# A decode step on one core: wider PV matmuls, the first FFN weight as the moving operand, the second as rows only

## The chip, the core and the metric

The kernel runs on one core of one Trainium2 chip. The time is that of the device, in microseconds (us). TensorE is called PE (its weight loads PEld), VectorE DVE, ScalarE ACT, GpSimd POOL, and SyncE, which issues the transfers, SP (its queue SPq).

## The reference

Eight batch rows of one token (D = 448) pass through attention, a SiLU block, the same attention and the same SiLU block again, with residuals and LayerNorm without weights. Attention has 16 query heads on 8 key-value heads (head width 256) over the last 1024 of 4096 cached positions; the FFN width is 1792. All inputs are bf16.

```python
def _A_ref(x, k_cache, v_cache, wq, wo):
    ...
    W = min(4096, max(256, Sk // 4))
    rep = Hq // Hkv
    q = (lambda x, *d: x.transpose(*d))((x @ wq).reshape(B, Sq, Hq, Dh), 0, 2, 1, 3)
    k = jnp.repeat(k_cache[:, :, Sk - W:, :], rep, axis=1)
    v = jnp.repeat(v_cache[:, :, Sk - W:, :], rep, axis=1)
    scores = jnp.einsum("bhqd,bhkd->bhqk", q, k) * (Dh ** -0.5)
    p = _softmax(scores, axis=-1)
    o = jnp.einsum("bhqk,bhkd->bhqd", p, v)
    return (lambda x, *d: x.transpose(*d))(o, 0, 2, 1, 3).reshape(B, Sq, Hq * Dh) @ wo
...
x = A_x
x = x + _A_ref(_layernorm(x, axis=-1), A_k_cache, A_v_cache, A_wq, A_wo)
x = x + _B_ref(_layernorm(x, axis=-1), B_w1, B_w2)
x = x + _A_ref(_layernorm(x, axis=-1), A_k_cache, A_v_cache, A_wq, A_wo)
x = x + _B_ref(_layernorm(x, axis=-1), B_w1, B_w2)
```

`_B_ref` is `silu(x @ w1) @ w2`.

## The kernel before

Both attention calls read the same keys and values, so each batch row's cache (8 key and 8 value blocks of 512 KB) is brought in once and used twice. SP loads the blocks as 256 transfers of 256 KB, in the order keys, values, batch by batch, into 29 slots of SBUF. A transfer waits for the landing of the one seven before it (`AHEAD = 7`) and for its slot to be free. Key slots of a batch become free after its second layer's scores, value slots after its second layer's PV. The weights follow the first batch's values.

The outer loop runs over the eight batches; for each, `layer1(b)` and `layer2(b)` declare tasks, and a planner (`Plan.schedule`) orders all tasks of each engine by a list schedule with assumed durations. The order is then fixed: each engine runs its list in order and waits by semaphores. Where PE would be idle, the planner puts `fill` matmuls (L1045) that change nothing. So the second half of one batch runs among the first half of the next.

The steps of a batch, with the names that the profile and the change use:

- **KT** (L998, DVE): turns the key blocks 32 x 32 in place, 16 pieces of 512 words per batch.
- **scores** (L672, PE), the max over positions and its spread (L678 to L691, DVE), **exp** (L695, ACT), **pT** (L701, PE) and its copy (L709, ACT), the sums **l** over positions by eight matmuls with a matrix of ones (L712, PE), their reciprocal **rl** (L717, DVE).
- **PV** (`pv_rows`, L731): p as stationary operand (two columns), a value block of 256 columns as moving operand, four heads side by side in the four 32-column tiles of the array, added up over the eight blocks of positions. Then the eviction **oev** (L736, ACT), the turn into columns **oT** (L738, PE) and the division (L742, DVE).
- **wo** (`rows_part`, L774, and `cols_part`, L780): output product as rows in four tiles, the rest as columns; **fold** (L790 ACT, L791 PE) adds the four row tiles to the columns in bank YB.
- **up** (`up`, from L830): `xb_evac` (L801, L802), the statistic **s12** (`stat`, L808 to L813: four matmuls for the sum, four for the squares, one for epsilon), then DVE's reciprocal root (`rsqrt`), and **w1** (L833): 14 blocks of 128 x 128 of the weight as stationary operand, x as moving operand of 32 equal columns, for four parts of D. `vt`, `tanh`, `zh`, `hT` give silu.
- **chain** (`chain`, from L847): **w2** 8 parts as rows and 6 as columns, fold, the normalized row `xn`, the second statistic (its root on POOL), **wq** (L877) in four tiles, its turn **qT** (L882, DVE), `qsel` (L888, PE), `qbd` (L892, DVE); then the second layer's scores.

PSUM is used by whole banks: a task that writes a bank waits for all readers of that bank. `rowb`, the row that `fold` reads, is the first half of the buffer `qT`; the second layer's `e_sb` is its second half. The second layer's last FFN is done for seven batches at once in `final_rows` and for the last batch in `final_last`.

Of the kernel before, what the change touches and what calls it, by code (L numbers as in the profile page):

```python
# [280 lines left out]
def bass_interleave_layers__sliding_block_cached__dense_activation_silu__decode_kernel(  # L281
# [15 lines left out]
    F0 = 1024  # L297
# [33 lines left out]
    pT_sb = [sb(f"pT_sb{i}", [P, 2, 4, 16], BF16) for i in range(2)]  # L331
# [5 lines left out]
    o_sb = [sb(f"o_sb{i}", [P, DH], BF16) for i in range(2)]  # L337
# [9 lines left out]
    rowb = qT[:, 0:256].bitcast(BF16)  # L347
    ROWK = [("qT", 0)]
# [4 lines left out]
    xbt = sb("xbt", [P, KC + 1], BF16)  # L353
# [36 lines left out]
    C_L, C_O, C_Q, C_ST = 256, 320, 352, 480  # L390
    C_CV = 256
    C_XF = 256
    C_W1 = 64
# [3 lines left out]
    def bk(i):  # L397
        return [("bank", i)]
# [53 lines left out]
    pool(lambda e: e.memset(xbt[:], 0.0), [], [("xbt", i) for i in range(3)], 0.1)  # L452
# [14 lines left out]
    pool(lambda e: e.memset(w1_sb[64:128, 3 * F + F - F0:], 0.0), [], ["w1_pad"], 0.2)  # L467
# [25 lines left out]
    def load_w1():  # L493
        for c in range(3):
            dma(lambda e, c=c: e.dma_start(w1_sb[:, c * F:(c + 1) * F], B_w1[c * P:(c + 1) * P, :]),
                [("w1", c)], P * F * 2, "w1%d" % c)
        for h in range(2):
            n = (F0, F - F0)[h]
            dma(lambda e, h=h, n=n: e.dma_start(w1_sb[64 * h:64 * h + 64, 3 * F:3 * F + n],
                                                B_w1[3 * P:D, h * F0:h * F0 + n]),  # L500
                [("w1", 3 + h)], D3 * n * 2, "w1%d" % (3 + h))
# [16 lines left out]
    W1_R = [("w1", c) for c in range(5)] + ["w1_pad"]  # L518
# [19 lines left out]

    def w1_l(o, i):
        g, a = o // 2, o % 2  # L540
        c = i * F + g * 2 * P if i < 3 else 3 * F + (g % 4) * 2 * P
        return w1_sb[:, c + a:c + 2 * P:2]
# [104 lines left out]

    def sums_w1():
        pe(proj(STB, 0, range(FC), range(KC), w1_l, lambda o, i: xb0[:, part(i, o >= 8), NB:NB + 1], CW, wide=True),
           XB0 + X1 + W1_R, bk(STB), (CW, 1), "cs1")  # L650
        dve(lambda e: e.tensor_copy(cs1[:], bank[STB][:, 0:FC * CW:CW]), bk(STB), ["cs1"], 0.2)
# [30 lines left out]
    def softmax(b, layer, ks):  # L682
# [17 lines left out]
        for k2 in ks:  # L700
            pe([lambda e, uh=uh, ql=ql, k2=k2: e.matmul(  # L701
                bank[lb][64 * ql:64 * ql + 64, (k2 * 4 + uh) * 16:(k2 * 4 + uh) * 16 + 16],
# [7 lines left out]
            pT_sb[ei][:, k0:k1].rearrange("p k u n -> p (k u n)"), bank[lb][:, k0 * 64:k1 * 64], ACTF.Copy),  # L710
# [6 lines left out]
        dve(lambda e: e.reciprocal(rl_sb[ei][:, 8 * k0:8 * k1], bank[lb][:, C_L + 8 * k0:C_L + 8 * k1]), bk(lb),  # L717
            [("rl", ei, k) for k in ks], 0.25, "rl%d" % layer)

    def p_col(ei, k2, j, qh, uh):  # L720
        return pT_sb[ei][:, k2, uh, j * 4 + qh * 2:j * 4 + qh * 2 + 2]

    def pv_rows(b, layer, k2, oT_dst, oT_key, ob, oi, c0, nj=4):
        lb, ei = LB[layer], layer
        for qh in range(2):
            for u2 in range(2):
                fns = []
                for uh in (2 * u2, 2 * u2 + 1):
                    for j in range(nj):
                        vv = slots[slot_of[b, "v", 4 * k2 + j]][:, (qh * 4 + uh) * DH:(qh * 4 + uh + 1) * DH]  # L730
                        fns.append(lambda e, qh=qh, uh=uh, j=j, vv=vv: e.matmul(  # L731
                            bank[ob][32 * j:32 * j + 2, c0:c0 + DH], p_col(ei, k2, j, qh, uh), vv,
                            start=(qh == 0 and uh == 0), stop=(qh == 1 and uh == 3), tile_position=(0, 32 * j)))
                pe(fns, [("slot", slot_of[b, "v", 4 * k2 + j], qh) for j in range(nj)] + [("pT", ei, k2)], bk(ob),
                   (DH, 4), "PV%d.%d.%d" % (layer, b, k2))
        act(lambda e: e.activation(o_sb[oi][:], bank[ob][:, c0:c0 + DH], ACTF.Copy), bk(ob), [("o", oi)], 0.385,  # L736
            "oevh" if ob == OB[0] else "oev%d" % layer)
        pe([lambda e, a=a: e.matmul(  # L738
            bank[lb][:, C_O + (k2 * 2 + a) * 8:C_O + (k2 * 2 + a) * 8 + 8], o_sb[oi][:, a:DH:2],
            ident[:].rearrange("p (j r) -> p j r", j=4)[:, :, 0:2], start=True, stop=True) for a in range(2)],  # L740
           [("o", oi), "ident"], bk(lb), (8, 1), "oT%d" % layer)
# [58 lines left out]
    def xb_evac():  # L800
        act(lambda e: e.activation(xbt[:, 0:3], xcols()[:, 0:3], ACTF.Copy), bk(YB), [("xbt", 0)], 0.175, "xbt")  # L801
        act(lambda e: e.activation(xbt[:, 3:4], xcols()[:, 3:4], ACTF.Copy, scale=mask4[:, 3:4]), bk(YB) + MASK4,  # L802
            [("xbt", 1)], 0.175, "xbt")
# [278 lines left out]
```

## Time and profile before

| | us |
|---|---|
| median of 3 runs | 270.83 |
| lowest, highest | 269.54, 271.26 |
| profiled execution | 269.46 |
| its span, first to last instruction | 267.7 |

In the profile's rows, a group is: line, engine, operation, output <- input (partitions x elements, type), count | busy time, mean ns of one | idle time of the engine before them and what ended it. In the timeline each row has its start and its length in us. The clock that PE was granted is 0.968 of full on the mean: it was half in three stretches, about 49 to 55, 103 to 107 and 250 to 257 us.

| busy in the last 40 us (228 to 268) | us |
|---|---|
| PE | 36.56 |
| DVE | 14.24 |
| ACT | 11.22 |
| POOL | 2.02 |

### The profile page before, as it was taken

What the parts mean: (1) busy time and instruction counts of PE and PEld (TensorE: products, weight loads), DVE (VectorE), ACT (ScalarE), POOL (GpSimd) and SP (SyncE); (2) the same over time, 40 slices, a digit from 0 to 9 for tenths busy, and PEclk for the clock granted to TensorE, in tenths of its full rate; (3) what the DMA queues carried; (4) which work ended last, traced back from release to release, by engine and by line L of the source; (5) the groups of instructions that cost most, each with busy time, mean ns of one, the idle gap of its engine ahead of it and who ended that gap; (6) DMA issues with size and microseconds to landing.
All of it is one profiled execution on the core that took longest, in us unless ns stands there. A gap on an engine that the chain in (4) does not pass through costs nothing.

```text
span 267.7 us, 11667 instructions
## 1 busy us (share of the span) xinstructions
PE 210.4 (79%) x5178; PEld 135.7 (51%) x5178; DVE 153.8 (57%) x453; ACT 75.0 (28%) x259; POOL 21.0 (8%) x115
## 2 busy tenths in 40 slices
PE   0054684778789878987899889769889985999996
PEld 0052341354457545654566556446555752667763
DVE  7289110156927880986498479818773891334233
ACT  2004310211053314332432533143343312430322
POOL 6100000002000200020002001000200020003000
PEclk9999999689999997999999999999999999999689
DMA  6999999999999999997999998999999998100000
GB/s 248 343 403 392 385 333 401 319 334 354 351 351 298 373 349 348 376 366 249 353 382 348 315 369 296 375 303 354 383 311 337 343 351 272 39 6 2 5 2 4
DMA packets 41123, 78.44 MB, mean 293 GB/s; under 512 B 4321, under 2 KB 7345, under 8 KB 40689
## 3 DMA queue, kind: packets, MB, share of 16 engines
q1 hardware_dynamic: 41072, 77.69, 82.3%
q8 instruction: 41, 0.67, 1.0%
q14 instruction: 10, 0.07, 0.1%
HBM read 77.67 MB, written 0.01 MB: 290 GB/s over the span
## 4 chain that ended last, share of the span: by engine, by line
PE 41%; DMA 35%; DVE 9%; SPq 6%; ACT 5%; issue 3%; ACTq 0%
DMA slot<-in_A_k_cache_dram 24%; PE bank L731 7%; PE bank L672 7%; DMA slot<-in_A_v_cache_dram 6%; DMA w2o<-in_A_wo_dram 6%; PE bank L774 5%; PE bank L877 5%; DVE slot L998 5%; SPq L531 4%; PE bank L833 3%; PE bank L780 3%; PE bank L1045 2%; DVE qT L882 2%; PE bank L558 2%; PE bank L888 2%
## 5 line engine op out<-in xcount | busy, mean ns | idle before, releaser
L998 DVE STREAM_TRANSPOSE slot<-slot 128x512 uint32<-128x512 uint32 x128 | 81.7, 684 | 11.4 <-DMA slot<-in_A_k_cache_dram 11.4
L672 PE MATMUL bank<-slot,qbd 128*8 128x256 bf16 x1024 | 38.2, 283 | 9.1 <-DVE mseg L678 4.5
L731 PE MATMUL bank<-slot,pT_sb 128*2 128x256 bf16 x960 | 41.7, 297 | 3.8 <-DMA slot<-in_A_v_cache_dram 2.7
L672 PEld LDWEIGHTS bank<-slot,qbd 128*8 128x8 bf16 x1024 | 23.4, 86 | 19.9 <-DVE mseg L678 6.4
L1045 PE MATMUL bank<-wq_sb,cols_b 128*32 128x512 bf16 (+2 forms) x269 | 29.7, 422 | 0.0
L731 PEld LDWEIGHTS bank<-slot,pT_sb 128*2 128x2 bf16 x960 | 22.4, 88 | 12.3 <-issue 5.2
L656 ACT ACTIVATE qbd<-q1s 32x128 bf16<-32x128 bf16 x32 | 10.1, 314 | 51.6 <-PE bank L672 51.0
L717 DVE RECIPROCAL rl_sb<-bank 128x16 f32<-128x16 f32 x16 | 4.1, 256 | 33.1 <-PE bank L712 33.0
L736 ACT ACTIVATE o_sb<-bank 128x256 bf16<-128x256 f32 x32 | 12.3, 383 | 35.9 <-PE bank L731 20.1
L774 PE MATMUL bank<-w2o,oT 128*1 128x448 bf16 x256 | 15.6, 359 | 6.9 <-issue 4.3
L877 PE MATMUL bank<-wq_sb,xn 128*4 128x256 bf16 (+1 forms) x384 | 18.7, 307 | 1.4 <-issue 0.9
L790 ACT ACTIVATE qT<-bank 128x448 bf16<-128x448 f32 x17 | 9.3, 544 | 28.0 <-PE bank L774 28.0
L566 POOL TENSOR_SCALAR rstd<-va 128x1 int32<-128x1 int32 x8 | 1.5, 192 | 195.3 <-ACT va L823 195.3
L678 DVE TENSOR_REDUCE mseg<-bank 128x1 f32<-128x256 f32 x32 | 12.8, 405 | 6.2 <-PE bank L672 6.0
L882 DVE STREAM_TRANSPOSE qT<-bank 128x256 f32<-128x256 f32 (+1 forms) x24 | 11.9, 521 | 7.7 <-PE bank L877 7.7
L833 PE MATMUL bank<-xbt,w_sb 128*128 128x32 bf16 x504 | 15.8, 177 | 0.1
L833 PEld LDWEIGHTS bank<-xbt,w_sb 128*128 128x128 bf16 x504 | 14.0, 97 | 2.0 <-ACT xbt L801 1.7
L742 DVE TENSOR_TENSOR oT<-bank,rl_sb 128x16 bf16<-128x16 f32 (+1 forms) x32 | 6.0, 186 | 15.0 <-PE bank L738 14.9
L1045 PEld LDWEIGHTS bank<-wq_sb,cols_b 128*32 128x32 bf16 (+2 forms) x269 | 9.1, 105 | 8.4 <-issue 5.6
L774 PEld LDWEIGHTS bank<-w2o,oT 128*1 128x1 bf16 x256 | 5.3, 82 | 12.3 <-DVE oT L742 4.8
L819 DVE SCALAR_TENSOR_TENSOR va<-bank,m 128x1 f32<-128x1 f32 x9 | 1.3, 149 | 17.0 <-ACT m L817 16.8
L695 ACT ACTIVATE qT<-bank,mb,rstd 128x256 bf16<-128x256 f32 x16 | 8.7, 565 | 7.0 <-DVE mb L691 6.8
(164 smaller groups left out, 267.6 us busy)
## 6 DMA issues: line engine op xcount, KB each, us to landing
slot<-in_A_k_cache_dram SPq DMA_DIRECT2D x128, 256.0 KB, 5.3
slot<-in_A_v_cache_dram SPq DMA_DIRECT2D x128, 256.0 KB, 5.2
w2o<-in_A_wo_dram SPq DMA_DIRECT2D x2, 1792.0 KB, 12.7
wq_sb<-in_A_wq_dram SPq DMA_DIRECT2D x3, 1024.0 KB, 7.0
w2o<-in_B_w_dram SPq DMA_DIRECT2D x1, 1568.0 KB, 15.5
w_sb<-in_B_w_dram SPq DMA_DIRECT2D x3, 448.0 KB, 13.9
wq_sb<-in_A_wq_dram SPq DMA_DIRECT2D x2, 256.0 KB, 10.3
w_sb<-in_B_w_dram SPq DMA_DIRECT2D x1, 128.0 KB, 12.7
```

The lines of the kernel that those rows point to most:

```text
L531: dma(lambda e, h=h: e.dma_start(slots[s][:, 1024 * h:1024 * h + 1024], src[h]), [("slot", s, h)], W * DH, "slot%d_%d" % (s, h), rate=378e ...
L656: act(lambda e, q=q: e.activation(qbd[0][32 * q:32 * q + 32].rearrange("p k c (q r) -> p (k c) q r", r=2)[:, :, q, :], q1s[32 * t:32 * t + ...
L672: fns.append(lambda e, cb=cb, par=par, j=j, kvh=kvh, kv=kv: e.matmul(bank[sc][32 * j:32 * j + 8, k2 * 256:(k2 + 1) * 256], qbd[layer][:, k ...
L678: dve(lambda e: e.tensor_reduce(mseg[layer][:, k2:k2 + 1], bank[sc][:, k2 * 256:(k2 + 1) * 256], AX.X, ALU.max, negate=True), bk(sc), [("m ...
L731: fns.append(lambda e, qh=qh, uh=uh, j=j, vv=vv: e.matmul(bank[ob][32 * j:32 * j + 2, c0:c0 + DH], p_col(ei, k2, j, qh, uh), vv, start=(qh ...
L736: act(lambda e: e.activation(o_sb[oi][:], bank[ob][:, c0:c0 + DH], ACTF.Copy), bk(ob), [("o", oi)], 0.385, "oevh" if ob == OB[0] else "oev ...
L774: pe([lambda e, i=i, c=c: e.matmul(bank[XB][32 * c:32 * c + 1, 0:D], rhs(i), w_sb[:, i * D:(i + 1) * D], start=(first and i - i0 < 4), sto ...
L833: pe([lambda e, i=i, k=k, o=o: e.matmul(bank[XB][:, C_W1 + o * CW:C_W1 + o * CW + CW], w1_l(o, i), xbt[:, k:k + 1].broadcast_to([P, CW]), ...
L877: fns.append(lambda e, j=j, c=c, wb=wb, off=off, h0=h0, n=n, k2=k2: e.matmul(bank[wb][32 * j:32 * j + 4, h0:h0 + n], xn[:, part(c, k2), j, :],
L882: dve(lambda e, wb=wb, h0=h0, n=n: e.transpose(qT[:, h0:h0 + n].rearrange("p (c a i) -> p c a i", a=2, i=32), bank[wb][:, h0:h0 + n].rearr ...
L998: dve(lambda e, v=v: e.transpose(v, v), [("slot", s, h)], [("slot", s, h)], 0.67, "KT")
L1045: fills = {n: [lambda e, j=j, m=P // n: e.matmul(bank[OB[0]][m * j:m * j + m, 0:2 * DH], zero_b.broadcast_to([P, m]), wq_sb[:, 0:2 * DH], ...
```

## The change

Five edits in one.

1. **PV**: two value blocks (512 columns) move at once against four columns of p, so each pair of blocks also computes two products that aren't used; `oev` copies 512 columns, and `oT` picks the wanted rows with two matmuls where one stood. p is stored so that the columns of one head lie together. The output buffer of layer 1 is the first `e_sb`. In layer 2 the two halves now have a bank each (OB[1] and SC[1]); for the last batch its PV stays 256 wide.
2. **w1**: x is the stationary operand (one column, in `final_rows` seven) and the weight moves, 448 columns in each of four tiles; DVE turns the rows into columns (`turn`) into the buffer `qT`, and `vt` reads them there. The weight's last 64 rows are stored in two equal halves.
3. **w2**: rows that follow the new order of h (row 14 p + c), so that the load is one run per partition; all 14 parts are rows in `chain`, except in the last batch (8 and 6 as before).
4. **Sums**: l is one matmul over 64 or 128 columns and a reduction by DVE; s12 takes both sums with one matmul per part, by a column of ones stored beside x in `xbt`.
5. **wq**: 512 columns at once in both halves of the heads, except in the last batch.

```diff
-    F0 = 1024
+    F0 = F // 2
+    FN = F // 4
...
-    pT_sb = [sb(f"pT_sb{i}", [P, 2, 4, 16], BF16) for i in range(2)]
+    pT_sb = [sb(f"pT_sb{i}", [P, 2, 8, 4, 2], BF16) for i in range(2)]
...
-    o_sb = [sb(f"o_sb{i}", [P, DH], BF16) for i in range(2)]
+    o_sb = [e_sb[0][:].rearrange("p k u x -> p (k u x)"), sb("o_sb1", [P, 2 * DH], BF16)]
...
+    yT = qT[:].rearrange("p (h f) -> p h f", h=2)[:, :, 0:FN // 2]
...
-        dma(lambda e: e.dma_start(w2_sb[:, 0:FC * D].rearrange("p (c n) -> p c n", n=2 * D),
-                                  B_w2.rearrange("(c p a) n -> p c (a n)", p=P, a=2)), ["w2"], F * D * 2, "w2",
-            rate=375e3)
+        dma(lambda e: e.dma_start(w2_sb[:, 0:FC * D], B_w2.rearrange("(p c) n -> p (c n)", c=FC)), ["w2"], F * D * 2,
+            "w2", rate=375e3)
...
+    def w1_rows(bi, lhs, n, key_of, name):
+
+        for i, c0, c1 in ((0, 0, 4), (1, 0, 4), (2, 0, 4), (3, 0, 2), (3, 2, 4)):
+            k = part(i, c0 > 0)
+            pe([lambda e, i=i, k=k, c=c: e.matmul(
+                bank[bi][32 * c:32 * c + n, 0:FN], lhs(k),
+                w1_sb[:, i * F + c * FN:i * F + (c + 1) * FN] if i < 3 else
+                w1_sb[:, 3 * F + c % 2 * FN:3 * F + (c % 2 + 1) * FN],
+                start=(i == 0), stop=(i == KC - 1), tile_position=(0, 32 * c)) for c in range(c0, c1)],
+               key_of(k) + W1_R, bk(bi), (FN, 4), name)
+
+    def turn(bi, dst, reads, writes, name):
+
+        dve(lambda e: e.transpose(dst.rearrange("p h (j i) -> p h j i", i=32),
+                                  bank[bi][:, 0:FN].rearrange("p (i h j) -> p h j i", h=2, i=32)),
+            bk(bi) + reads, writes, 0.18 + FN / 950.0, name)
...
-        pe([lambda e, uh=uh, qh=qh: e.matmul(
-            bank[lb][:, C_L + 8 * k0:C_L + 8 * k1], ones_b[:],
-            pT_sb[ei][:, k0:k1, uh, :].rearrange("p k (j q r) -> p k j q r", j=4, q=2)[:, :, :, qh, :],
-            start=(uh == 0 and qh == 0), stop=(uh == 3 and qh == 1)) for uh in range(4) for qh in range(2)],
-           [("pT", ei, k) for k in ks] + ["ones_b"], bk(lb), (16, 1), "l%d" % layer)
...
+        pe(lambda e: e.matmul(bank[lb][:, C_L:C_L + 64 * nk], ones_b[:],
+                              pT_sb[ei][:, k0:k1].rearrange("p k n u r -> p (k n u r)"), start=True, stop=True),
+           [("pT", ei, k) for k in ks] + ["ones_b"], bk(lb), (64 * nk, 1), "l%d" % layer)
+        rl = rl_sb[ei][:, 8 * k0:8 * k1]
+        dve(lambda e: e.tensor_reduce(
+            rl.rearrange("p (n r) -> p n r", r=2),
+            bank[lb][:, C_L:C_L + 64 * nk].rearrange("p (n x r) -> p n r x", r=2, x=8), AX.X, ALU.add), bk(lb),
+            [("ls", ei, k) for k in ks], 0.3, "ls%d" % layer)
...
-                            bank[ob][32 * j:32 * j + 2, c0:c0 + DH], p_col(ei, k2, j, qh, uh), vv,
-                            start=(qh == 0 and uh == 0), stop=(qh == 1 and uh == 3), tile_position=(0, 32 * j)))
+                            bank[ob][32 * j:32 * j + 2 * w, 0:w * DH], p_col(ei, k2, j, qh, uh, w), vv,
+                            start=(qh == 0 and uh == 0), stop=(qh == 1 and uh == 4 - w), tile_position=(0, 32 * j)))
...
+        pe([lambda e, a=a, i=i: e.matmul(
+            bank[lb][:, C_O + (k2 * 2 + a) * 8:C_O + (k2 * 2 + a) * 8 + 8],
+            o_sb[oi][:, i * DH + a:(i + 1) * DH:2],
+            ident[:].rearrange("p (j r) -> p j r", j=4)[:, :, 2 * i:2 * i + 2], start=(i == 0), stop=(i == w - 1))
+            for a in range(2) for i in range(w)], O_K[oi] + ["ident"], bk(lb), (8, 1), "oT%d" % layer)
...
-        pe([lambda e, c=c: e.matmul(s1, ones_b[:], xbt[:, c:c + 1].broadcast_to([P, XW]),
-                                    start=(si == 1 and c == 0), stop=(c == KC - 1), skip_group_check=True)
+        s2, s1, s12 = (bank[bi][:, c0 + u:c0 + v] for u, v in ((0, XW), (XW, 2 * XW), (0, 2 * XW)))
+        pe([lambda e, c=c: e.matmul(s12, xbt[:, c, 0:1].broadcast_to([P, P]),
+                                    xbt[:, c, :].unsqueeze(2).broadcast_to([P, 2, XW]),
+                                    start=(si == 1 and c == 0), stop=False, skip_group_check=True)
...
+        w1_rows(XB, lambda k: xbt[:, k, 0:1], 1, lambda k: [("xbt", max(0, k - 2))], "w1")
+        turn(XB, yT, [], QT0[0:1] + QT1, "w1T")
...
-        rows_part(0, 8, True, True, w2_sb, lambda i: hT[:, i:i + 1], ["hT"] + W2_R, "w2r")
-        cols_part(range(8, FC), w2_l, lambda i: hT[:, i:i + 1], ["hT"] + W2_R, "w2c")
+        nr = 8 if tail else FC
+        rows_part(0, nr, True, True, w2_sb, lambda i: hT[:, i:i + 1], ["hT"] + W2_R, "w2r")
+        if tail:
+            cols_part(range(nr, FC), w2_l, lambda i: hT[:, i:i + 1], ["hT"] + W2_R, "w2c")
...
-            parts = [(XB, 0, DH), (YB, DH, DH)] if k2 == 0 else [(XB, 0, 2 * DH)]
+            parts = [(XB, 0, DH), (YB, DH, DH)] if tail and k2 == 0 else [(XB, 0, 2 * DH)]
...
-        for o0, o1 in ((0, 4), (4, 8), (8, 11), (11, 14)):
-            pe(proj(ya, o0 * nb, range(o0, o1), range(KC), w1_l, lambda o, i: xb8[:, part(i, o >= 8), :], nb),
-               ["xbt8"] + TFK + (["xbt84", "xbt84z"] if o0 >= 8 else []) + W1_R, bk(ya), (nb, 1), "w18")
+        w1_rows(ya, lambda k: xb8[:, k, :], nb, lambda k: (["xbt84", "xbt84z"] if k == KC else ["xbt8"]) + TFK, "w18")
...
+            ob = SC[1] if k2 else OB[1]
             if last:
-                pv_rows(b, 1, k2, oT1, "oT1", OB[1], 1, DH if k2 else 0)
+                pv_rows(b, 1, k2, oT1, "oT1", ob, 1, w=1)
             else:
-                pv_rows(b, 1, k2, oT2[:, :, :, b], ("oT2", b), OB[1], 1, DH if k2 else 0)
+                pv_rows(b, 1, k2, oT2[:, :, :, b], ("oT2", b), ob, 1)
```

More of the change, by code (lines that the diff above doesn't have):

```diff
@@ L517, in bass_interleave_layers__sliding_block_cached__dense_activation_silu__decode_kernel @@
     WQ_R = [("wq", c) for c in range(5)]
-    W1_R = [("w1", c) for c in range(5)] + ["w1_pad"]
+    W1_R = [("w1", c) for c in range(5)]
     slot_of = {}
@@ L734, in pv_rows @@
                 pe(fns, [("slot", slot_of[b, "v", 4 * k2 + j], qh) for j in range(nj)] + [("pT", ei, k2)], bk(ob),
[L735 to L741, printed above, removed]
+                   (w * DH, 4), "PV%d.%d.%d" % (layer, b, k2))
@@ new lines, in pv_rows @@
+        act(lambda e: e.activation(o_sb[oi][:, 0:w * DH], bank[ob][:, 0:w * DH], ACTF.Copy), bk(ob), O_K[oi],
+            0.2 + w * 0.2, "oevh" if ob == OB[0] else "oev%d" % layer)
+        pe([lambda e, a=a, i=i: e.matmul(
[3 more added lines that the diff above has]
+            for a in range(2) for i in range(w)], O_K[oi] + ["ident"], bk(lb), (8, 1), "oT%d" % layer)
@@ L828, in up @@
         xb_evac()
[L829 removed]
+        act(lambda e: e.activation(xbt[64:128, 4, 0:1], xbt[0:64, 3, 0:1], ACTF.Copy), [("xbt", 1)], [("xbt", 2)], 0.2, "x4")
         stat(YB, C_S1, 4.0, 0)
[L831 to L839 removed]
+        w1_rows(XB, lambda k: xbt[:, k, 0:1], 1, lambda k: [("xbt", max(0, k - 2))], "w1")
+        turn(XB, yT, [], QT0[0:1] + QT1, "w1T")
+        dve(lambda e: e.scalar_tensor_tensor(
+            out=vt[:].rearrange("p (h j) -> p h j", h=2), in0=cs1[:].rearrange("p (h j) -> p h j", h=2),
+            scalar=nmean[:, 0:1], in1=yT[:, :, 0:FN // 2:32], op0=ALU.mult, op1=ALU.add),
+            QT0[0:1] + QT1 + ["cs1", "nmean"], ["vt"], 0.2, "vt")
         if pad:
```

80 lines of the change are left out of this document (33 added, 47 removed).

## The prediction

> **What bounds the kernel now.** I read the page's busy shares, its chain and its DMA part first, then the DMA view and the waits of the DMA queue over 62 to 222 us, then the timeline of one batch and of the tail. The time is 270.83 us (median of three, 269.54 to 271.26); the profiled execution took 269.46 us with a span of 267.7, so 1.8 us lie around the span and it stands 1.37 under the median.
>
> ```profile
> span 267.7 us, 11667 instructions
> PE 210.4 (79%) x5178; PEld 135.7 (51%) x5178; DVE 153.8 (57%) x453; ACT 75.0 (28%) x259; POOL 21.0 (8%) x115
> DMA  6999999999999999997999998999999998100000
> GB/s 248 343 403 392 385 333 401 319 334 354 351 351 298 373 349 348 376 366 249 353 382 348 315 369 296 375 303 354 383 311 337 343 351 272 39 6 2 5 2 4
> PE 41%; DMA 35%; DVE 9%; SPq 6%; ACT 5%; issue 3%; ACTq 0%
> q8 instruction: 41, 0.67, 1.0%
> ```
>
> No engine is full, but the transfer row reads 9 for 34 slices, to about 227 us, and the chain is shared by PE and DMA. So there is a stream of about 225 us that must pass, then a tail of some 40 us with no transfers. Within the stream the rate falls from about 400 GB/s to about 345 although the row stays at 9. The last line says what else uses the DMA engines: 41 packets of instructions, 0.67 MB, that is 16 KB each. PE has 5178 matmuls and as many weight loads, 10,356 together, 253 for each packet; the other engines have 453, 259 and 115. So nearly all of these packets are PE's own program.
>
> ```profile
> 16.00:24.00 8.00, 4.23 (x118) 3.32 (x115) 7.90 (x15) 2.77 (x8) 0.00 (x0) 1.00 1.05 404
> 62.00:222.00 160.00, 138.74 (x3522) 89.08 (x3512) 114.04 (x311) 51.78 (x182) 13.48 (x70) 0.99 0.98 343
> q1 hardware_dynamic: 29837, 54.33, 96.7%
> q8 instruction: 28, 0.46, 1.1%
> slot<-in_A_v_cache_dram SPq DMA_DIRECT2D x109, 256.0 KB, 5.2
> slot<-in_A_k_cache_dram SPq DMA_DIRECT2D x98, 256.0 KB, 5.3
> ...
> SPq L531 <- PE bank L877: 5.8, 4, 2.1
> SPq L525 <- PE bank L731: 1.4, 5, 0.4
> SPq L525 <- PE bank L780: 1.2, 1, 1.2
> ```
>
> The first two rows are stretches (length, busy time and count of PE, PEld, DVE, ACT, POOL, clock, DMA share, GB/s). While few matmuls run, the stream goes at 404 GB/s; VectorE is full then, so VectorE's work is not what slows it. From 62 to 222 us 54.33 MB pass, which at 404 GB/s would take 134.5 us; 25.5 us are lost. Two things can hold them: 28 instruction packets (one for 251 of PE's 7034 instructions there), each of 1.1% x 16 engines x 160 us / 28 = 1.0 us on its engine; and the waits of the transfer queue for PE to free a slot, 8.4 us in the three rows. If these overlap wholly with the packets' stalls, a packet costs the stream 25.5 / 28 = 0.91 us; if not at all, 0.61. [...] A look at one such place:
>
> ```profile
> q8 instruction: 1, 0.02, 2.3%
> ...
> SPq L525 <- DMA slot<-in_A_v_cache_dram: 2.6, 4, 1.8
> ...
> q8 instruction: 8, 0.13, 1.4%
> ```
>
> Between 76 and 78.5 us one packet takes 2.3% x 16 x 2.5 = 0.9 us, and in 76 to 80 the queue's four waits for a landing hold one of 1.8 us. The packets are thus on the path. (The last line is the tail's, 228 to 268 us.) The 207 transfers in that stretch are 6.5 batches of 32; a batch lasts 160 / 6.5 = 24.7 us.
>
> The second bound is the chain of a batch: PV and output product, first FFN product, second, query product, scores; the scores free the key slots that the transfer queue waits for. The four waits above, in 6.5 batches, say that about half of the batches are held by it.
>
> **Part 1, PE's program (gain).** Per batch the edit removes these matmuls, each with its weight load: 40 of w1 (56 to 16), 60 of PV (28 in layer 1, 32 in layer 2), 18 of w2 (32 to 14), 16 of wq, 14 of the sums l, 8 of the two statistics, and adds 8 for the wider oT: 148. That is 296 instructions x 6.5 / 251 = 7.7 packets fewer of 28. A packet's cost to the stream: 0.06 (a sixteenth of 1.0, if it holds one engine and the others run on) to 0.91; I take 0.75, the middle of 0.61 and 0.91, since the place shown is of that size. Gain 5.8 us (0.5 to 7.0). Before 62 us lie 5 more packets (41 less 28 and the tail's 8); 28% fewer, 1.4 at 0.75, give 1.0 us. The one w2 load in long runs in place of 1792-byte ones I cost at nothing: the wide loads around it take the same engines for the same bytes; at most some tenths.
>
> [...]
>
> **Part 2, the batch's chain (loss).**
>
> ```profile
> 136.86 1.20 PE L833 MATMUL bank<-xbt,w_sb 128*128 128x32 bf16 x42
> 137.58 0.12 DVE L819 SCALAR_TENSOR_TENSOR va<-bank,m 128x1 f32<-128x1 f32 x1
> 138.51 0.22 DVE L838 SCALAR_TENSOR_TENSOR vt<-cs,nmean,bank 128x14 f32<-128x14 f32 x1
> 138.65 0.15 DVE L577 SCALAR_TENSOR_TENSOR rstd<-nt,rstd 128x1 f32<-128x1 f32 x1
> 139.41 0.55 PE L774 MATMUL bank<-w2o,hT 128*1 128x448 bf16 x8
> 139.89 0.76 PE L780 MATMUL bank<-hT,w2o 128*128 128x16 bf16 x24
> 140.61 0.26 PE L791 MATMUL bank<-cols_b,qT 128*128 128x16 bf16 x4
> ...
> L882 DVE STREAM_TRANSPOSE qT<-bank 128x256 f32<-128x256 f32 x16 | 6.2, 428 | 5.6 <-PE bank L877 5.6
> L882 DVE STREAM_TRANSPOSE qT<-bank 128x512 f32<-128x512 f32 x8 | 5.7, 708 | 2.0 <-PE bank L877 2.0
> L877 PE MATMUL bank<-wq_sb,xn 128*4 128x512 bf16 x128 | 9.8, 378 | 0.0
> L877 PE MATMUL bank<-wq_sb,xn 128*4 128x256 bf16 x256 | 8.9, 272 | 1.4 <-issue 0.9
> L736 ACT ACTIVATE o_sb<-bank 128x256 bf16<-128x256 f32 x32 | 12.3, 383 | 35.9 <-PE bank L731 20.1 <-PE bank L738 15.5
> L790 ACT ACTIVATE qT<-bank 128x448 bf16<-128x448 f32 x17 | 9.3, 544 | 28.0 <-PE bank L774 28.0
> 263.24 0.92 PE L774 MATMUL bank<-w2o,hT 128*1 128x448 bf16 x14
> ```
>
> w1: 256 more columns cost a matmul 378 - 272 = 106 ns, so 448 take about 186; four groups of four side by side take 0.74 us where 56 took about 1.5 (42 of them 1.20). But VectorE, not PE, ends this stage: from va at 137.58 to the last rstd step at 138.80 it runs a row of small dependent steps, and vt lies among them. The new turn of 448 columns is 428 + 192/256 x 280 = 638 ns on the same engine. In the wait for va it costs little, inside the row all of it: 0 to 0.64, I take 0.6, as VectorE works off K transposes ahead of va. The statistic has four matmuls fewer before va: 0.1 back. w2: now 8 as rows, their eviction hidden behind 24 as columns, fold 1.20 us after the start (139.41 to 140.61). All 14 as rows take 0.92 (the last row), then the eviction of 0.54 (448 columns, L790) lies open: 0.92 + 0.54 + 0.05 = 1.51, so 0.3 later. PV: the eviction of 512 columns is 544 + 64 x 161/192 = 598 ns in place of 383, 0.2 later, once on the chain; the matmuls stream the same columns. wq: one turn of 708 for two of 428, after as many columns: 0. The sums' reduction on VectorE (bounded by the 160 ns of eight columns and the 405 of 256 in the max steps' kind of work) runs beside PV; where PV's cover is gone it is 0.3. The query rows' new sharing of their buffer with the turn makes the turn wait for layer 2's pT of the batch before; that is early in the order except in the last batch.
>
> ```profile
> L678 DVE TENSOR_REDUCE mseg<-bank 128x1 f32<-128x256 f32 x32 | 12.8, 405 | 6.2 <-PE bank L672 6.0
> L686 DVE TENSOR_REDUCE mg<-mT 128x2 f32<-128x8 f32 x16 | 2.6, 160 | 0.5
> 117.79 0.83 issue
> 191.23 0.89 issue
> PEld bank L738 <- issue: 4.2, 16, 0.4
> ```
>
> Together +1.0 per batch. Against it stand PE's stalls for no shown reason (the two longest in the chain, 0.8 to 0.9; 28% fewer instructions save about 0.15 a batch) and matmuls of the sums, statistics and wq that leave PE's queue (0.2 of the 0.6 us they take). Net +0.65 (0 to 1.0), charged to half of 6.5 batches: 2.1 us.
>
> [...]
>
> **Part 3, the tail.**
>
> ```profile
> 249.54 0.56 PE L558 MATMUL bank<-slot,w_sb 128*128 128x7 bf16 x16
> 250.03 1.88 PE L731 MATMUL bank<-slot,pT_sb 128*2 128x256 bf16 x32
> 251.84 1.23 PE L558 MATMUL bank<-slot,w_sb 128*128 128x7 bf16 x40
> ```
>
> Two turns on the path (+1.2) and one wide eviction (+0.2); the 7-row product w1, 1.79 us between the PV halves, falls to 0.74 at full clock or 1.5 at half (-0.6), and sums and stalls give 0.3 back: +0.5.
>
> **Sum.** -5.8 + 2.1 - 1.0 + 0.5 = -4.2: 265.3 against 269.46, 266.6 against the median; I put 266.
>
> **Rivals.** Slower: the chain sets every batch. The slot waits then appear in all 6.5 batches, with 1.0 each, and the faster stream only waits longer: 6.5 + 0.5 - 1.0, about 276. It decides once the wait for PE before V loads exceeds 2 us in most batches. For it: DVE is at 114 of 160 us and gets 1.2 us more per batch. Against: half of the batches have no such wait now. Chance 0.24, with 273 to 277. No change: instruction packets are hidden and the chain's additions fall into waits for transfers: 269.5 to 270.5; against it stands the stall at 76 us. 0.16. More: each packet at 0.91 and the half-clock stretch of the tail gone (PV at 1.88 where four tiles of 32 matmuls stream in about 0.9): 258 to 261, 0.10. The forecast has 0.50, 262 to 269.
>
> One per cent is about what a measurement can tell. Faster by over 1% (below 268.1): 0.46 + 0.10 = 0.56; within: 0.18; slower: 0.26. The range 259 to 275 leaves out the ends of both outer cases; the forecast's own is 262 to 269.
>
> **What would show it.** PE's count near 3,900 and instruction packets near 31; the rate from 62 us on above 355 GB/s; the transfer stream ending near 222 us. hT 0.5 us later after its statistic, fold 0.3 later after w2's start. The queue's waits for PE much longer than 8 us would speak for the slower rival; an unchanged rate with fewer packets for "hidden".

## The result and the profile after

The changed kernel takes 260.86 us (median of four runs, 258.98 to 262.15), the kernel before beside it 270.19 us (267.34 to 271.26). The ratio is 0.9665, with a 95% interval of 0.9563 to 0.9767: faster by 3.4%, 9.3 us between the medians. The profiled execution took 260.01 us with a span of 258.2. Medians and ranges here are of all executions, while ratios leave out those more than 1.5% above the fastest of their kernel; where that left a single one of the kernel before (e9 to e11), no ratio is given.

The page of the changed kernel, the lines that answer to those of before:

```profile
span 258.2 us, 9306 instructions
PE 199.1 (77%) x3974; PEld 104.0 (40%) x3992; DVE 163.0 (63%) x472; ACT 79.8 (31%) x260; POOL 20.6 (8%) x115
PEclk9999999979999999999999999999999999999998
q8 instruction: 31, 0.51, 0.7%
DMA 59%; PE 22%; DVE 8%; ACT 4%; SPq 4%; issue 2%; ACTq 0%; DVEq 0%
```

PE lost 1204 matmuls and ten packets of instructions. The chain of waits has turned over: transfers carry 59% of it where they carried 35%, PE 22% where it carried 41%, and "issue" fell from 3% to 2%. The changed kernel from 60 to 216 us, one stretch of the same view as before (length, then busy time and count of PE, PEld, DVE, ACT, POOL, clock, DMA share, GB/s):

```profile
60.00:216.00 156.00, 131.63 (x2648) 66.45 (x2653) 119.09 (x320) 55.49 (x182) 13.21 (x69) 1.00 1.01 356
```

The rate rose from 343 to 356 GB/s in this execution. The last value load was issued at 225.09 us before and at 216.66 after (the timeline of the transfer queue): 8.4 of the 9.5 us by which the span shrank are won in the stream, 1.1 behind it. Executions differ: a second profile of the changed kernel (e1, 265.15 us) has 347 GB/s over the same 156 us and its last value load at 220.08 us.

The waits of the transfer queue for PE in the changed kernel, 60 to 216 us (total us, times, longest):

```profile
SPq L530 <- PE bank L894: 4.1, 3, 1.7
SPq L524 <- PE bank L749: 2.4, 6, 1.2
SPq L530 <- PE bank L684: 1.9, 1, 1.9
```

These three rows add up to the 8.4 us of the three rows of before, but both sets are only the longest. Over all rows in which the queue waits for PE it is 11.0 us before (62 to 222 us) and 13.0 us here: the waits grew. The chain of one batch, its timeline in the changed kernel (start, length):

```profile
106.19 0.92 PE L646 MATMUL bank<-w_sb,xbt 128*1 128x448 bf16 x14
...
108.90 0.12 DVE L837 SCALAR_TENSOR_TENSOR va<-bank,m 128x1 f32<-128x1 f32 x1
108.94 0.63 DVE L655 STREAM_TRANSPOSE qT<-bank 128x448 f32<-128x448 f32 x1
...
110.92 0.17 DVE L860 SCALAR_TENSOR_TENSOR hT<-th,zh 128x14 bf16<-128x14 f32 x1
...
111.14 0.92 PE L793 MATMUL bank<-w2o,hT 128*1 128x448 bf16 x14 [0.81 <-DVE hT L860]
...
112.11 0.54 ACT L809 ACTIVATE qT<-bank 128x448 bf16<-128x448 f32 x1 [1.23 <-PE bank L793]
...
112.70 0.26 PE L810 MATMUL bank<-cols_b,qT 128*128 128x16 bf16 x4 [0.45 <-ACT qT L809]
```

The terms of the chain came as worked out. The turn runs right behind va, ahead of the row of small steps; from va to hT it is 2.02 us where it was 1.60 (137.58 to 139.18). The fold starts 1.56 us after w2, where it was 1.20. Two groups of the changed kernel confirm the sizes of the wide eviction and the turn (busy us, mean ns):

```profile
L655 DVE STREAM_TRANSPOSE qT<-bank 128x448 f32<-128x448 f32 x10 | 6.4, 639 | 2.7 <-PE bank L646 2.7
...
L754 ACT ACTIVATE e_sb<-bank 128x512 bf16<-128x512 f32 x16 | 9.6, 597 | 15.6 <-PE bank L749 13.0 <-PE bank L756 2.5
```

The tail: first the stretch of before at half clock, then two of the changed kernel.

```profile
250.00:256.80 6.80, 6.80 (x135) 4.20 (x132) 2.10 (x13) 0.77 (x2) 0.00 (x0) 0.50 0.01 2
```

```profile
216.70:240.00 23.30, 22.30 (x500) 13.46 (x502) 8.87 (x35) 6.90 (x24) 2.16 (x12) 1.00 0.15 48
240.00:256.80 16.80, 13.65 (x299) 8.09 (x297) 7.39 (x39) 5.36 (x18) 0.00 (x0) 1.00 0.01 2
```

Before, 6.8 us of the tail ran at a clock of 0.50; in this execution only the last 1.4 us did. So the chain became longer by about what was forecast, and the stream shorter by more. What had to be found is whether packets on the DMA engines are the cause.

### The profile page after: what moved, and what is told of

Its sections match the earlier page's. It is cut to its first block, busy times and chain, and to the rows that moved or that the text cites. A ratio compares the mean times of both kernels' runs of the same rounds, so it can differ in the third digit from the quotient of the medians.

```text
span 258.2 us, 9306 instructions
## 1 busy us (share of the span) xinstructions
PE 199.1 (77%) x3974; PEld 104.0 (40%) x3992; DVE 163.0 (63%) x472; ACT 79.8 (31%) x260; POOL 20.6 (8%) x115
## 3 DMA queue, kind: packets, MB, share of 16 engines
q1 hardware_dynamic: 40304, 77.69, 84.4%
## 4 chain that ended last, share of the span: by engine, by line
DMA 59%; PE 22%; DVE 8%; ACT 4%; SPq 4%; issue 2%; ACTq 0%; DVEq 0%
DMA slot<-in_A_k_cache_dram 28%; DMA slot<-in_A_v_cache_dram 23%; DMA w2o<-in_B_w_dram 6%; PE bank L684 3%; PE bank L749 3%; PE bank L894 3%; PE bank L793 3%; SPq L497 2%; DMA wq_sb<-in_A_wq_dram 2%; PE bank L1063 2%; DVE slot L1015 2%; PE bank L552 1%; PE bank L905 1%; PE bank L646 1%; ACT qT L809 1%
## 5 line engine op out<-in xcount | busy, mean ns | idle before, releaser
L1015 DVE STREAM_TRANSPOSE slot<-slot 128x512 uint32<-128x512 uint32 x128 | 81.3, 682 | 12.8 <-DMA slot<-in_A_k_cache_dram 12.8
L749 PE MATMUL bank<-slot,pT_sb 128*4 128x512 bf16 (+1 forms) x512 | 40.2, 378 | 1.3 <-ACT pT_sb L722 1.0
L894 PE MATMUL bank<-wq_sb,xn 128*4 128x512 bf16 (+1 forms) x272 | 18.0, 366 | 0.3
L749 PEld LDWEIGHTS bank<-slot,pT_sb 128*4 128x4 bf16 (+1 forms) x512 | 11.4, 83 | 14.4 <-ACT pT_sb L722 4.2
L730 DVE TENSOR_REDUCE rl_sb<-bank 128x16 f32<-128x128 f32 x16 | 4.6, 288 | 18.0 <-PE bank L726 17.9
L899 DVE STREAM_TRANSPOSE qT<-bank 128x512 f32<-128x512 f32 (+1 forms) x17 | 11.5, 680 | 5.6 <-PE bank L894 5.4
L754 ACT ACTIVATE e_sb<-bank 128x512 bf16<-128x512 f32 x16 | 9.6, 597 | 15.6 <-PE bank L749 13.0
L1063 PEld LDWEIGHTS bank<-wq_sb,cols_b 128*32 128x32 bf16 (+2 forms) x329 | 10.3, 103 | 9.3 <-issue 5.7
L905 PE MATMUL bank<-qT,irep 128*128 128x64 f32 x32 | 7.4, 321 | 6.3 <-DVE qT L899 6.3
L646 PE MATMUL bank<-w_sb,xbt 128*1 128x448 bf16 x144 | 12.1, 376 | 0.1
L754 ACT ACTIVATE o_sb<-bank 128x512 bf16<-128x512 f32 (+1 forms) x16 | 9.1, 567 | 8.5 <-PE bank L749 5.8
L713 PE MATMUL bank<-ident,e_sb 128*64 128x16 bf16 x128 | 4.9, 184 | 8.5 <-ACT e_sb L707 8.0
```

The source lines that it names most:

```text
L646: pe([lambda e, i=i, k=k, c=c: e.matmul(bank[bi][32 * c:32 * c + n, 0:FN], lhs(k), w1_sb[:, i * F + c * FN:i * F + (c + 1) * FN] if i < 3 else
L749: fns.append(lambda e, qh=qh, uh=uh, j=j, vv=vv: e.matmul(bank[ob][32 * j:32 * j + 2 * w, 0:w * DH], p_col(ei, k2, j, qh, uh, w), vv, star ...
L754: act(lambda e: e.activation(o_sb[oi][:, 0:w * DH], bank[ob][:, 0:w * DH], ACTF.Copy), bk(ob), O_K[oi], 0.2 + w * 0.2, "oevh" if ob == OB[ ...
L894: fns.append(lambda e, j=j, c=c, wb=wb, off=off, h0=h0, n=n, k2=k2: e.matmul(bank[wb][32 * j:32 * j + 4, h0:h0 + n], xn[:, part(c, k2), j, :],
L899: dve(lambda e, wb=wb, h0=h0, n=n: e.transpose(qT[:, h0:h0 + n].rearrange("p (c a i) -> p c a i", a=2, i=32), bank[wb][:, h0:h0 + n].rearr ...
L1015: dve(lambda e, v=v: e.transpose(v, v), [("slot", s, h)], [("slot", s, h)], 0.67, "KT")
```

## The experiments

**First set, seven deep: the packets.** e1 is the changed kernel again. e2 undoes one edit that costs PE instructions and no columns; e3 and e4 add instructions on GpSimd alone.

```diff
e2
-    def pv_rows(b, layer, k2, oT_dst, oT_key, ob, oi, nj=4, w=2):
+    def pv_rows(b, layer, k2, oT_dst, oT_key, ob, oi, nj=4, w=1):
e3 (e4: 512), in the loop that emits the program
+                    if e == "pool" and t.name == "rowpad":
+                        for _ in range(256):
+                            eng.wait_ge(handles["act"], 1)
```

> The changed kernel again, as the measure for the three runs beside it. All theories: ratio to the kernel before 0.960 to 0.975, profiled execution 259 to 262 us, 31 instruction packets on q8.

> Layer 1 and 2 products with V go back to one value block of 256 columns at a time; everything else stays as changed. 52 matmuls a batch come back (28 in layer 1, 32 in layer 2, less 8 of the output turn; none in the last batch's layer 2), the columns streamed stay the same, the chain of a batch gets about 0.2 us shorter (eviction of 256 instead of 512 columns). Theory 1 (each instruction packet of PE holds up the stream of transfers by about 0.75 us): 52 x 2 x 7.5 / 252 = 3.1 packets more, 34 in all, 2.3 us slower than the changed kernel. Theory 2 (the gain came from PE's time: shorter products, earlier slots): PE's columns are the same, so 0 to -1 us. Theory 3 (the gain came from the granted clock, the half-clock stretches at 103 to 107 and 250 to 257 us gone): slower only if such a stretch returns, and then by 2 to 3 us at that place.

> The changed kernel, and behind the last GpSimd task of each batch 256 waits on GpSimd for a semaphore value that was long reached: 256 x 64 B = 16 KB of program a batch, 128 KB in all, on an engine that is busy 8% and stands on no chain. PE's program is the changed kernel's. Theory 1: 8 packets of 16 KB (or 16 of half the size) more on the DMA engines, 6 to 7 of them in the stream, each 0.75 us if it costs what one of PE's does: 3.5 to 6 us slower; half of that if GpSimd's blocks are fetched in smaller packets. Theory 2 and 3: 0, since neither PE's work nor its clock changes.

> As the run before with 512 waits a batch, 32 KB of program a batch. Theory 1: twice the loss of the run before, 6 to 12 us slower than the changed kernel, unless a packet costs nothing on GpSimd. Theory 2 and 3: 0. If this one is slower and the run before is not, it is GpSimd's own time (its task of a batch coming late behind 512 waits) and no packet.

Measured, with the kernel before at 270.48 us: e1 261.15 us, ratio 0.9658 (0.9578 to 0.9738); e2 263.90, 0.9722 (0.9646 to 0.9798), 34 packets; e3 269.78, 1.0003 (0.9923 to 1.0083); e4 289.07, 1.0725 (1.0664 to 1.0786). e2 fits 0.75 us a packet, but its interval overlaps with that of e1, and its profile has another account: PE has 3.1 us of "issue" waits in 60 to 212 us where e1 has 0.7, and two half-clock stretches of 3.4 us, from 74.2 and 84.4 us, where e1 has none between 60 and 220. e3 and e4 fall out as tests of the sum: 256 waits hold GpSimd for 11.3 us, and in the tail a task on the path stands behind them. They also bring less program than was meant: the trace of e3 has 1024 semaphore instructions more for its 2048 waits, two waits in each, so 64 KB and not 128: 8 packets of 8 KB more on q14 than in e1, 64 bytes for each of the 1024. The first row is of e3's waits; then the stretch of 60 to 222 us of e3 and of e1:

```profile
POOL slot L933 <- issue: 11.3, 1, 11.3
```

```profile
60.00:222.00 162.00, 135.37 (x2717) 68.54 (x2726) 120.77 (x324) 56.99 (x184) 13.38 (x70) 1.00 0.99 350
```

```profile
60.00:222.00 162.00, 134.26 (x2686) 67.75 (x2699) 119.99 (x321) 56.78 (x186) 13.37 (x70) 1.00 0.99 347
```

The stream itself ran at 350 GB/s with eight more packets (17 against 9 on q14, of 8 KB each) and at 347 without: GpSimd's packets, half as large and on another queue, cost it nothing that shows.

**Second set: depth, one engine, filler.** The new rival, theory 1b, was that all of PE's packets load one DMA engine.

```diff
e5
-    AHEAD = 7
+    AHEAD = 10
e6 (e7: 121 in place of 120): four loads of a batch in two pieces
+        cut = 120 if h == 0 and kvh % 4 == 3 else P
+        dma(lambda e: e.dma_start(dst[0:cut], src[0:cut]), [("slot", s, h)], ...
+        if cut < P:
+            add("sp", lambda e: e.dma_start(dst[cut:P], src[cut:P]), writes=[("cut", s, h)], ...
e8
-  ... for j in range(n)] for n in (1, 2, 4)}
+  ... for j in range(1)] for n in (1, 2, 4)}
```

> The changed kernel with transfers ten deep instead of seven (each waits for the landing of the tenth before it). From 60 to 216 us the changed kernel moves 55.5 MB in 156 us with 21 of PE's packets of 0.93 us; 55.5 MB at the 404 GB/s of 16 to 24 us of the kernel before take 137.4 us, so 18.6 us are lost, 0.89 for each packet; for the kernel before it was 25.5 / 28 = 0.91. Theory 1 (as in the forecast: a packet keeps one DMA engine for 0.9 us and the seven-deep queue then stops the other fifteen): three more transfers in flight are 1.9 us more of work for the fifteen, so most of a packet's stall is covered, 5 to 12 us faster than the changed kernel. Theory 1b (all of PE's packets pass through the same one of the 16 DMA engines, which also has its sixteenth of the stream to move: the stream lasts as long as this engine's share and packets together): depth is no help, 0 to -2 us. Theory 2 (PE's time, not packets): 0 to -1 us.

> Four of a batch's 32 loads (first half of key and value heads 3 and 7) are cut into one of 120 rows and one of 8 rows. [...] Theory 1 and 2: 0 to +3 us (four more issues a batch).

> [...]

> A filler (the matmuls against zero columns that keep the clock up) issues one matmul where it issued two or four side by side: about 230 of the 311 filler matmuls go, with a weight load each, 460 instructions or 1.8 packets of 256; the planned order of all other work stays. Theory 1 and 1b: 1.5 us faster than the changed kernel, 29 packets in all. Theory 2: 0 to -0.5 us. Theory 3 (clock): slower by 2 to 5 us if fewer columns of the array no longer keep the clock up, with a half-clock stretch in the profile.

Measured, with the kernel before at 270.79 us: e5 256.55, ratio 0.9618 (0.9556 to 0.968); e6 273.93, 1.0271 (1.0174 to 1.0367); e7 275.66, 1.0302 (1.0183 to 1.0421); e8 261.17, 0.9702 (0.9507 to 0.9898). The DMA view of e5 from 48 to 90 us:

```profile
DMA packets 8478, 16.51 MB, mean 393 GB/s; under 512 B 943, under 2 KB 955, under 8 KB 8376
...
q8 instruction: 5, 0.08, 0.7%
```

Five of PE's packets lie in a stretch that runs at 393 GB/s. By theory 1b, one engine with a sixteenth of the stream and five packets of 0.93 us would allow 404 x (42 - 4.7) / 42 = 359, an estimate from these rows and the 404 GB/s of before. Theory 1b falls. The price of theory 1 falls as well, by stretches that hold no packet of PE's and no wait of the queue for a slot, from 2 us after the last packet on: one of the kernel before and two of the changed kernel seven deep, then one of the kernel before (e9, below) and one of e5 ten deep.

```profile
69.80:76.70 6.90, 4.30 (x94) 2.20 (x88) 5.21 (x15) 2.41 (x7) 0.00 (x0) 1.00 1.03 351
58.50:66.00 7.50, 6.89 (x134) 3.66 (x136) 5.97 (x11) 1.24 (x8) 1.91 (x10) 1.00 1.00 350
122.10:128.40 6.30, 6.07 (x111) 2.48 (x113) 2.95 (x11) 2.85 (x8) 0.00 (x0) 1.00 1.03 358
69.20:74.80 5.60, 3.02 (x68) 1.38 (x58) 4.05 (x13) 2.27 (x7) 0.00 (x0) 1.00 1.06 405
56.50:63.00 6.50, 6.00 (x125) 3.33 (x121) 5.74 (x10) 0.26 (x1) 1.91 (x10) 1.00 1.05 406
```

Seven deep the stream runs at 350 to 358 GB/s here with no packet near; ten deep it runs at 405. (Other such stretches of the seven-deep profiles lie between 296 and 375, those ten deep between 404 and 406.) Most of the 25.5 us that the forecast divided among packets and waits is therefore lost without either. At 351 GB/s the 54.33 MB take 154.8 of the 160 us, and the 5.2 us left, divided by 28 packets, are 0.2 us each (0.3 at 358 GB/s): an estimate, from few stretches, of what a packet can cost the stream, with nothing set aside for the waits. Seven transfers of 256 KB at 5.2 us from issue to landing, the forecast's row, are 353 GB/s, the rate itself, and three more in flight raise it with no packet involved: the depth sets it. Why a landing takes that long beside a busy kernel, when the stream went at 404 GB/s seven deep from 16 to 24 us, no run shows.

The gain of e5 was 4.6 us between the medians of two chips (0.9618 against 0.9658 of the kernel before beside each, with intervals that overlap), short of the 5 to 12 expected, since the stream then ran into the batches (transfer queue of e5, 60 to 212 us):

```profile
SPq L530 <- PE bank L894: 20.2, 5, 4.9
SPq L524 <- PE bank L749: 7.7, 9, 1.6
...
SPq L530 <- PE bank L684: 5.3, 5, 4.2
```

e6 and e7 lost 12.8 and 14.5 us against e1, beyond the 3 us that theories 1 and 2 gave e6 at most, and hardly differ though one splits a load at row 120 and the other at row 121: most likely the four extra issues of a batch are what costs. The two pieces were meant to take bytes off some of the engines; which engines they go to no run shows, and so neither run says where the packets go. Not all of the loss is the stream's: PE has 5.0 and 4.4 us of "issue" waits in them (60 to 212 us), where e1 has 0.7. e8 has 222 matmuls and one packet fewer (30), the time of e1 and a median clock of 0.988 (e1: 0.984); the 1.5 us expected did not show, within its own spread of 5.5 us (256.76 to 262.25).

**Third set, ten deep: with the stream at 405 GB/s where nothing holds it, what is the change still worth?** e9 is the kernel before with AHEAD = 10, e10 is e2 with it, e11 the changed kernel with it and this:

```diff
e11
-        nr = 8 if tail else FC
+        nr = 8
-        if tail:
+        if True:
             cols_part(range(nr, FC), w2_l, ...
```

> The kernel before the change with transfers ten deep. With ten in flight the changed kernel ran at 393 GB/s from 48 to 90 us with five packets of instructions in it (356 at seven deep), took 256.55 us, and its transfer queue then waited 34 us for PE to free slots (12 at seven deep): packets are covered there, and the chain of a batch sets the pace. Theory 1 (the change's worth is packets, and its chain is longer by the 0.65 to 1.0 us a batch of the forecast): the kernel before, with packets covered and the shorter chain, runs 3 to 6 us under the changed one at ten deep, 250 to 254 us, ratio to the kernel before 0.925 to 0.94. Theory 2 (the change made PE's work of a batch shorter): it stays 3 us or more above the changed one at ten deep, 260 to 268 us, ratio 0.96 to 0.99. Between the two (254 to 260 us): the change is worth nothing but its packets, and the chain's additions cancel against PE's savings.

> The changed kernel ten deep, with the products with V one block of 256 columns at a time: at seven deep this undoing cost 2.7 us (263.90 against 261.15) for three packets more. Theory 1: the three packets are covered at ten deep and the chain is 0.2 us a batch shorter, 0 to -1.5 us against the changed kernel at ten deep (256.55). Theory 2 (368 matmuls more on PE, 3.6 us more busy time): +2 to +4 us.

> The changed kernel ten deep, with w2 again 8 rows and 6 as columns in every batch (18 matmuls a batch more, one packet in all), so that the rows' eviction has columns beside it. By the forecast's term the fold comes 0.3 us earlier a batch. If the chain of a batch sets the pace at ten deep: 1.5 to 2.3 us faster than 256.55. If PE's time does: 18 matmuls of 27 to 32 ns are 0.5 us a batch, 0 to +3 us.

Measured on one chip, with the kernel before at 272.03 us (262.54 to 274.64): e9 276.74 (270.24 to 279.62), e10 263.90 (261.33 to 268.08), e11 255.44 (254.19 to 256.13). The changed kernel ten deep (e5) had 256.55 (255.82 to 257.72) on another chip, where the kernel before had 270.79. The ranges of e9, e10 and e5 do not overlap. No theory had said 20 us for e9 or 7 for e10. Theory 1 as written falls: with the stream freed, the kernel before is not ahead of the changed one but far behind. It is no faster than at seven deep either, so the stream alone was not what held it. The chain that ended last in e9 (profiled in an execution of 279.47 us, one of the two longest) says what does; its pieces called "issue" of over 0.5 us, time in which PE waited for nothing that is shown (start, length):

```profile
105.31 1.29 issue
110.85 2.25 issue
141.54 1.79 issue
161.16 1.08 issue
173.49 0.61 issue
188.20 1.15 issue
194.34 1.51 issue
```

Each has the end of a packet of PE's instructions 1.3 to 1.5 us before its own. From the trace's records of the packets:

```
e9: packet ends at     105.22  111.70  141.87  160.78  172.75  187.91  194.57
    PE goes on at      106.60  113.10  143.33  162.24  174.10  189.35  195.85
    later by             1.38    1.40    1.46    1.46    1.35    1.44    1.28
```

All seven go on 1.3 to 1.5 us after a packet has landed. The place in the program says the same. By the trace, PE had begun 3265, 3521, 4801, 5569, 6081, 6593 and 6849 instructions (matmuls, weight loads and semaphore instructions) when it stopped: each is a multiple of 256 plus 193, one and the same place in every 256, and a packet came for every 251 to 253 of PE's instructions (the forecast's count). The reading that fits both is that PE had run out of program and waited for its next packet. Around the second one, the timeline of PE in e9:

```profile
109.33 1.20 PE L833 MATMUL bank<-xbt,w_sb 128*128 128x32 bf16 x42
110.46 0.39 PE L731 MATMUL bank<-slot,pT_sb 128*2 128x256 bf16 x7
113.10 1.23 PE L731 MATMUL bank<-slot,pT_sb 128*2 128x256 bf16 x17 [2.25 <-issue]
```

The DMA view of 110.7 to 111.8 us, and the stretches:

```profile
q8 instruction: 1, 0.02, 5.0%
```

```profile
109.60:110.85 1.25, 1.25 (x45) 0.93 (x42) 1.07 (x7) 0.26 (x2) 0.00 (x0) 1.00 1.11 424
110.85:113.05 2.20, 0.00 (x0) 0.00 (x0) 2.05 (x7) 0.31 (x1) 0.00 (x0) 1.00 0.55 202
113.05:116.45 3.40, 3.35 (x55) 1.96 (x55) 0.36 (x1) 0.87 (x2) 0.00 (x0) 0.50 0.49 136
```

Read in order: the 56 narrow matmuls of w1 use up 112 instructions in some 1.7 us (42 of the matmuls in 1.20), PE stops in the middle of a row of equal PV matmuls, a packet passes, PE goes on 1.4 us later, and then runs 3.4 us at half clock. The transfer rate falls to 202 and 136 GB/s beside it, because no slot comes free (the queue waits 5.9 us for PV there). The half-clock stretches of e9 last 3.4, 6.8 and 13.7 us. Four of its seven begin within 4 us of such a stall (113.0, 143.7, 164.2 and 191.5 us); the other three (58.4, 181.3 and 259.8 us) follow none of the seven.

How much each kernel waits like this is in the waits of PE, 60 to 212 us, rows "issue". Those of e9:

```profile
PE bank L731 <- issue: 3.8, 2, 2.3
PE bank L672 <- issue: 2.4, 2, 1.8
PE bank L780 <- issue: 1.3, 2, 1.1
PE bank L774 <- issue: 1.3, 1, 1.3
PE bank L712 <- issue: 1.1, 1, 1.1
PE bank L811 <- issue: 0.4, 1, 0.4
```

Sums: 10.3 us in e9, 6.2 in e10, 1.4 in e5, none in e11, 3.5 in the kernel before and 0.2 in the changed one at seven deep. e10's 52 matmuls a batch more were meant to be free at ten deep; they were paid for here, with half-clock stretches at 72.9, 158.3 and 209.5 us where e5 has none before its tail. e11, with 18 matmuls a batch more than e5 but no such stall and a clock of 0.997, is the fastest kernel of the study. Its 1.1 us against e5 fall between the two expectations, and chip and medians leave room for either. Depth and each edit enter the planner, so every run has an order of its own; none holds the order fixed, and part of a difference may be the order's.

**Last: the clock by itself**, seven deep, in the kernel before.

```diff
e12
-    def schedule(self, filler=None, look=0.3, dma_lat=2.0, target=4500.0, ...
+    def schedule(self, filler=None, look=0.3, dma_lat=2.0, target=6500.0, ...
-  ... for j in range(n)] for n in (1, 2, 4)}
+  ... for j in range(1)] for n in (1, 2, 4)}
```

> The kernel before the change, seven deep, with more filler on PE: the filler plans for 6500 columns in 3.41 us instead of 4500, and issues one matmul where it issued two or four (which alone left time and clock of the changed kernel as they were: 261.17 against 261.15 us, 0.988 against 0.984). 161 filler matmuls in place of 269, so about one packet less; all other work is the kernel's before. Theory 3 (the granted clock: 0.943 to 0.954 is the median of the kernel before over the runs so far, 0.984 that of the changed one; over executions of one kernel 0.01 of clock goes with 0.8 to 2.3 us): the clock rises to 0.975 or more and the time falls by 3 to 7 us, to 264 to 267 us. Theory 1 (packets): 0.75 us faster at most, 269 to 271. Theory 2 (PE's own work holds the batch): more filler stands before real work, 0 to +4 us, whatever the clock.

Measured: 265.84 us (261.76 to 270.66) against 269.47, ratio 0.9891 (0.9765 to 1.0016); the median clock of its executions is 0.965, that of the kernel before beside it 0.949. That is the 3 to 7 us of theory 3, at its low end, with a clock short of the 0.975 expected and an interval that just holds 1: it points to the clock and does not prove it. The profile still has 6.9 us of "issue" waits of PE in 60 to 212 us and 40 packets, so with more filler the median clock stood 0.016 higher, and the stalls stayed.

## Why the prediction came out as it did

The forecast was 266, its own range 262 to 269, the whole range 259 to 275; 260.86 lies in the last, and the sign was right. Step by step:

- **Counts.** PE 3974 (near 3,900), packets 31 (near 31): as worked out. The rate was 356 (above 355) in this execution and 347 in that of e1.
- **Part 1, "a packet's cost to the stream", 0.75 us.** Here the step failed. The price came from dividing all of the lost 25.5 us among 28 packets and the waits, and that a packet holds up the whole stream for that long no run shows. But seven deep the stream is that slow with no packet near (350 to 358 GB/s against 404), and by the estimate above 0.2 to 0.3 us a packet are left, 1.5 to 2.3 us of the 5.8. The 1.8 us wait at 76 us was a single place. And the kernel before gained nothing from a stream at 405 GB/s (e9), so a faster stream alone did not make it faster. What the traces do show beside packets is a loss of PE's time: in e9 PE stood still for 0.6 to 2.25 us at seven places, each time until 1.3 to 1.5 us after a packet had landed, and four half-clock stretches begin within 4 us of one. The forecast had two stalls of this kind in its hands, the rows "117.79 0.83 issue" and "191.23 0.89 issue", and booked them as stalls "for no shown reason", worth 0.15 us a batch. The five longest in the chain of before all end 1.3 to 1.4 us after a packet (the packets end at 57.74, 87.92, 117.27, 157.02 and 190.81 us), and PE had begun 1217, 2497, 3777, 5569 and 7105 instructions when it stopped, again 193 more than a multiple of 256:

```profile
58.76 0.36 issue
88.69 0.60 issue
117.79 0.83 issue
157.96 0.50 issue
191.23 0.89 issue
```

- **Part 2, the chain, 2.1 us in all.** The terms were right: turn 639 ns (638), va to hT 0.42 later (0.6 for the turn, 0.5 for hT), fold 0.36 later (0.3), wide eviction 597 ns (598). w1 was not: 0.92 us for 14 of its 16 matmuls against 0.74 for all, but VectorE ends that stage. Whether the charge came up is open: the queue's waits for PE rose by 2.0 us (11.0 to 13.0), the size of the charge, and yet the stream ended 8.4 us sooner.
- **Part 3, the tail, +0.5.** It came out at -1.1 in the profiled execution and at +0.7 in that of e1 (43.3 us from the last value load to the end, 42.6 before). The two turns lie there; the 6.8 us at half clock are gone in the first, and e1 has 3.4 us of half clock at 221.5 us. The rival "More" had named this stretch and 258 to 261; its other half, each packet at 0.91 on the stream, is against the stretches without packets.
- **Stream, -5.8 - 1.0 + 2.1 = -4.7 against -8.4.** The 6.8 us of packets are 1.8 to 2.7 by the same estimate (9.1 fewer, 0.2 to 0.3 each), and the chain's charge may have been paid. So most of the 8.4 us came from elsewhere. What lies at hand is PE: 3.3 us fewer "issue" waits, no 3.4 us at half clock from 103.2 us, and 1204 matmuls fewer to run; its share of the chain fell from 41% to 22%. No run parts these. That the time fell into the whole range is thus partly luck: the largest term was priced for a cause that the traces do not bear out, and gains that the forecast put at little took its place.
- **The slower rival.** Its condition, waits of over 2 us before the value loads in most batches, holds only ten deep (20.2 us in 5 waits), and there e5 is still the faster by far: the longer chain never outweighed fewer instructions.
- **"Hidden".** The rival "No change" had the packets hidden. For the stream that is nearer to the traces than part 1 was (0.2 to 0.3 us a packet by the estimate above, where part 1 had 0.75). For PE most are hidden too: the chain of the changed kernel has no such piece of over 0.32 us, beside 31 packets. But in e9 it does not hold, with seven of 0.6 to 2.25 us, the longest behind the 56 narrow matmuls of w1.

What stays open is how the 9.3 us split at seven deep between stalls, clock, PE's own work and the little that packets cost the stream. The profiles of e9 and e10 show the stalls clearly; at seven deep they are smaller and differ from one execution to the next. That a half-clock stretch follows from a stall is argued from their order in time, not shown by a run that removes one and keeps the other. At seven deep it does not even hold for the two stretches that the changed kernel's profile lacks: ahead of the one from 103.2 us PE waited 1.7 us for ScalarE, and ahead of the one from 250.0 us it was busy for 3.23 of 3.45 us.

## What to carry to other kernels

When a profile lists "issue" waits of PE, lay the times of its instruction packets beside them: if PE goes on a fixed time after a packet has landed (1.3 to 1.5 us here) and each such stop lies at one place in every 256 instructions, it has most likely run out of program; the longest stall here, 2.25 us in e9, came right behind 56 matmuls of 32 columns in some 1.7 us. Cut the count of PE's instructions first where narrow matmuls crowd together, as w1 did here. Only then deepen the transfers: depth ten gave the changed kernel some 4.6 us between medians and the kernel before nothing (276.74 against 272.03). And before you charge lost transfer time to something that passes beside the stream, read the rate in stretches where it does not pass.

## What the hardware showed beyond that

- PE went on 1.3 to 1.5 us after the end of a packet's transfer in each of these twelve stalls of the kernel before, at both depths, and each began at a multiple of 256 plus 193 of its instructions.
- Without packets or waits for slots near, 256 KB transfers ran at 350 to 358 GB/s seven deep (296 to 375 over all such stretches) and at 404 to 406 ten deep in these kernels.
- Two waits of GpSimd on a value long reached share an instruction and take 88 ns (11.3 us for 256 waits), and GpSimd's program came in packets of 8 KB on another queue, which left the stream as it was (350 GB/s with eight more of them, 347 without).
- Four loads of a batch cut in two slowed the kernel by far more than their bytes: 12.8 us over eight batches, 0.4 us for each extra issue. Why was not tried.
- The granted clock of a whole execution moved between 0.931 and 0.980 for the kernel before on a single chip, with times from 273.83 down to 262.54 us.
